# Start of a delta-rule and two-MoE kernel: loads on one queue, weight conversion ahead, unread products between small stages

## The chip, the cores and the metric

One core of a Trainium2 chip. The metric is the device time of one execution in microseconds (us); lower is better. The kernel before takes 1189.48 us, the median of three runs.

## The reference, cut to what matters

```python
# attention: batch 4, 8 heads, 768 positions, head size 48
k_n = k / (norm(k) + 1e-06)
for t in range(S):
    y[:, :, t] = einsum('bhd,bhde->bhe', q[:, :, t], state)
    v_old = einsum('bhde,bhd->bhe', state, kt)
    state = state + bt * einsum('bhd,bhe->bhde', kt, vt - v_old)
# the output, 3072 tokens x 384, goes through two MoEs
h = maximum(x @ w_in, 0.0); x = h * h @ w_out                # 384 -> 2048 -> 384
g = x @ w_gate; x = silu(g) * (x @ w_val) @ w_out2           # 384 -> 1536 -> 384
```

The weights come in 64-bit floats, everything else in 32-bit floats.

## The kernel before, in words

**Attention by blocks.** The 768 positions are 6 blocks J of 128, each of two chunks c of 64. The heads of all batches lie in two groups p. For a chunk the products of all keys (`gram`, ps_g, L360/361) are masked and scaled to a matrix M (L372, L379), and the inverse of one plus M gives the chunk's new values. For block 0 M is built in the tile NT and sent by `d_move` to the scratch d_scr (L392) and back as T (L396), where VectorE inverts 16x16 blocks (`invert16`, L474/L483); the result goes home to NT (L385, L394). TensorE then merges blocks to 32 and 64: `d_tr` (dt, ps_dt, L518), `d_merge1` (d1, ps_d), `d_merge2` (d2, ps_e), `tr11` (t11, ps_tq), `merge1` (m1, ps_m), `merge2` (m2, ps_x). After that `uu` (u, ps_u) makes the new values, `yy` (y, ps_y, L638/641) the outputs, `ku` (ps_s) the next state, and `ks` (ps_k) takes the old state's share from the values of the second chunk. `a_gram` (ps_a, L430) makes the products of queries and keys, masked by VectorE into AQ (L439). ScalarE and VectorE copy each small result from PSUM. Outputs are copied to a tile ys (L647), written to the scratch xs_scr (L650), and read back as xr by `fetch_x` (L665), for one half (256 tokens) at a time; `split_x` makes of it xh and xl (L673, L675). For blocks from 1 on, POOL inverts 32x32 blocks (`invert`, L453/L460) of M written out by `m_out` (L415) and read by `t_load` (L420).

The norms of K: `k_squares` squares on ScalarE into ps_sq and sums on VectorE (L335); `k_root` takes a root on ScalarE (L342) and eight small operations on VectorE (L344 to L351).

**Weights.** A weight is used as two pieces, hi and lo. `load_piece` (L145) loads 768 KB of raw words; ScalarE takes an absolute value (L171), VectorE does four steps on 128x768 words (L178, L180, L184, L189), ScalarE writes hi (L202), and VectorE or POOL writes lo as raw minus hi (L205). There are 16 such jobs for the first MoE, in the order w_in, w_out of a pair of column blocks m. `conv_to` does steps until a count is reached, `need` calls it before a product that wants a piece. A converted tile takes the buffer of a raw piece converted before.

**MoE units.** A unit is (J, tokens, m): ps_h (L794), ReLU and squares on ScalarE, hl on VectorE (L804), then ps_y (L820). Block 0 begins with 16 half-width units (8 values of m for each half of the tokens), all others are 512 tokens wide. Between units run the attention stages of the next block, from a list with times in units (`timed`; `spread` sets the stages of block 0's second chunk over units 0 to 5, those of `L2` over 5 to 12). Each layer takes three terms, hi times hi, hi times lo and lo times hi, so nine products a unit.

**Orders.** TensorE's and SP's instructions run in the order of the code; so do those of VectorE, POOL and ScalarE up to the first unit, and those of VectorE after it. The code's start is a list of `run`, `run_all` and `stage` calls, which fixes what stands behind what on each engine.

**Buffers.** Masks M and ys share two buffers (tag "xr"); the squares of K and, from the first unit on, ps_h share two banks (tag "h").

Of the kernel before, what the change touches and what calls it, by code (L numbers as in the profile page):

```python
# [20 lines left out]
def delta_attention_moe_moe2_kernel(  # L21
# [252 lines left out]
    def conv_to(steps, lo):  # L274

        while converted() < min(steps, STEPS * NCONV) and (making or conv1[0] in loaded or conv1[0] in begun):
            conv_one(lo)

    def need(m, kd):

        i = 2 * (m // 2) + kd + (1 if (m // 2, kd) == LAST and m % 2 else 0)
        conv_to(STEPS * (i + 1), nc.vector)
        if converted() < STEPS * (i + 2):
            flush()

# [96 lines left out]
    def d_move(c, out):
        mats = d_scr[c].rearrange("a g x s t -> (a g x) (s t)"), T0[c * 64:c * 64 + 64].rearrange("p a b -> p (a b)")
        if not out:
            nc.sync.dma_start(out=mats[0], in_=mats[1])  # L385
        for g in range(2):
            for a in range(2):
                p0 = g * 64 + a * 32
                rows = NT2[c][p0:p0 + 32, :, a * 32:(a + 1) * 32]
                blocks = d_scr[c, a, g].rearrange("x s t -> s x t")  # L390
                if out:
                    nc.sync.dma_start(out=blocks, in_=rows)  # L392
                else:
                    nc.sync.dma_start(out=rows, in_=blocks)  # L394
        if out:
            nc.sync.dma_start(out=mats[1], in_=mats[0])  # L396

    def gram(J, c, p, pool=False):
        ps = ps_t.tile([128, 8, 64], F32, tag="t", name="ps_g")
# [541 lines left out]

    def conv(n, lo=nc.vector):

        conv_to(converted() + int(STEPS * n), lo)

    P2 = range(2)

# [10 lines left out]
    for b0 in (0, 64):  # L958
# [1 line left out]
            out=mask[b0:b0 + 64], in_=mask[b0:b0 + 64], compare_op=ALU.is_ge, fill=1.0,  # L960
            base=0, pattern=[[-1, 64]], channel_multiplier=1,
        )
    for c in P2:
        k_load(1, c, nc.gpsimd)
    q_load(0, nc.gpsimd)
    run(("sq", 0, 0))
    run_all(("gram0", 0, 0, p) for p in P2)
    run(("root", 0, 0))
# [1 line left out]
    run(("mb0", 0, 0, 1, nc.gpsimd))  # L970
    run_all(("m0", 0, 0, p) for p in P2)
    run(("dmove", 0, True))
    load_w1(0, 0, nc.gpsimd)
    run(("sq", 0, 1))
    run_all(("gram0", 0, 1, p) for p in P2)
    run(("root", 0, 1))
    run(("mb0", 0, 1, 0, nc.vector))
    run(("mb0", 0, 1, 1, nc.gpsimd))
    run_all(("m0", 0, 1, p) for p in P2)
    run(("dmove", 1, True))  # L980
    load_w1(0, 1, nc.gpsimd)
    make_identity(nc, ident)
    for c in P2:
        v_load(0, c, nc.gpsimd)
    for p in P2:
        nc.gpsimd.memset(RSF[p], 0.0)
    run(("sq", 1, 0))
    load_w1(1, 0)
    run(("inv0", 0))
    run(("dmove", 0, False))  # L990
    run_all(("gram0", 1, 0, p) for p in P2)
    stage("agram", 0, 0)

    nc.vector.reduce_sum(lower, ident.rearrange("p (b z k) -> p z b k", z=2, k=16)[:, 1], axis=AX.XY)
    run(("inv0", 1))
    run(("dmove", 1, False))
    load_w1(1, 1)
    run(("root", 1, 0))
    run(("sq", 1, 1))
    run(("root", 1, 1))  # L1000
    run_all(("mb0", 1, 0, p, nc.gpsimd) for p in P2)
    merge16("dt", 0)
    run_all(("m0", 1, 0, p) for p in P2)
    run_all(("mout", 1, 0, p) for p in P2)
    merge16("d1", 0)
    run(("vn", 0, 0, nc.vector))
    run_all(("gram0", 1, 1, p) for p in P2)
    merge16("d2", 0)
    run_all(("mb0", 1, 1, p, nc.gpsimd) for p in P2)
    run_all(("m0", 1, 1, p) for p in P2)  # L1010
    run_all(("mout", 1, 1, p) for p in P2)
    run_all(("tload", 1, c) for c in P2)
    load_w1(2, 0)
    stage("t11", 0, 0)
    conv(0.5)
    stage("m1", 0, 0)
    run(("inv", 1, 0, 1, nc.gpsimd))
    conv(0.5)
    merge16("dt", 1)
    stage("m2", 0, 0)  # L1020
    conv(0.5)
    stage("u", 0, 0)
    merge16("d1", 1)
    stage("y", 0, 0)
    run(("fetch", 0, 0, TOK // 2))
    load_w1(2, 1)
    merge16("d2", 1)
    conv(0.5)
    stage("ku", 0, 0)
    stage("t11", 0, 1)  # L1030
    load_w1(3, 0)
    conv(0.5)
    run(("vn", 0, 1, nc.vector))
    stage("ks", 0, 1)
    stage("m1", 0, 1)
    stage("agram", 0, 1)
    load_w1(3, 1)
    conv(1)
    stage("m2", 0, 1)
    conv(0.5)  # L1040
    PRE = converted()
    order.close()
    order.enter_context(tc.manual_schedule(engines={mybir.EngineType.DVE, mybir.EngineType.Pool}))
# [13 lines left out]
    if True:  # L1057

        LOW2 = 300
        MID = 12  # L1060
        END = 7
        N1 = 10
        N2 = 99
        CR = 1.0
        RATE = 0.8
        LASTN = HMS[0] + 1
        seq = []
        for J in range(NJ):
            seq += [(J, c0, HT, m) for c0 in (0, HT) for m in range(HMS[J])]
            seq += [(J, 0, TOK, m) for m in range(HMS[J], NM1)]  # L1070
        L = chunk(["u"], 0, 1)
        L += [("ku", 0, 1, 0), ("y", 0, 1, 0), ("ku", 0, 1, 1), ("y", 0, 1, 1), ("fetch", 0, HT, HT)]
        L2 = [("loadq", 1), ("v", 1, 0), ("mback", 1, 0), ("mback", 1, 1), ("gap",), ("nout", 1), ("nback", 1, 0)]
        L2 += [("vn", 1, 0)] + loads(2)
        mid = MID
        GA = (5, 6, 9, 10)
        PG = []
        AA = (2, 5)
        NA = (2, 4)
        TA = 2  # L1080
# [128 lines left out]
```

## Time and profile before

| | |
|---|---|
| median of three runs | 1189.48 us (1186.06 to 1189.81) |
| the profiled execution, its own time | 1185.92 us |
| its span | 1184.1 us |
| mean granted TensorE clock | 0.946 |
| busy: PE, DVE, ACT, POOL | 92%, 55%, 33%, 23% |

The profile is one execution. "Busy" is the time an engine works; time in brackets behind a row is how long it had stood, and what ended that. The clock of TensorE is given as a share of full speed (2.4 GHz); 0.50 is the lower level, 1.2 GHz. Times of a row are from the span's start.

### The profile page before, as it was taken

The page shows a single profiled execution, that of the slowest core. Times are in us where ns is not written, and L with a number is a line of the kernel's source. Part 1 is how long each engine was busy: PE and PEld are TensorE (multiplying, and loading weights), DVE is VectorE, ACT ScalarE, POOL GpSimd, SP SyncE. Part 2 cuts the span into 40 slices and gives each one's busy share as a digit, 9 for nine tenths or more (in the row PEclk, how much of TensorE's full clock was granted, in tenths as well). Part 3 has the DMA queues.
Part 4 walks back from the last instruction along what each step waited for, and adds up shares of the span by engine and source line. Part 5 has one row for each costly group of instructions (what it writes and reads, how often), then busy time and mean ns, then how long its engine had stood idle before and what let it go on. Part 6 is the DMA issues. An engine that isn't in the chain of part 4 may idle for free. (4 is left out here: it accounts for less than half of the span.)

```text
span 1184.1 us, 25132 instructions
## 1 busy us (share of the span) xinstructions
PE 1087.6 (92%) x10863; PEld 905.3 (76%) x10863; DVE 645.5 (55%) x1116; ACT 385.2 (33%) x711; POOL 271.3 (23%) x394
## 2 busy tenths in 40 slices
PE   4378778999999999999999987899999999999998
PEld 4367667777888888788888865688888888888887
DVE  3859995456547546555543699834334343343333
ACT  1034563332233233323333666422122122122222
POOL 5067100480183166128000233300000000000000
PEclk8557887999999999999999999999999999999999
DMA  8537440461434326132211445301001010010000
GB/s 237 132 81 280 93 104 20 95 160 43 91 66 115 77 49 168 46 69 59 77 29 27 161 143 177 107 1 54 1 1 54 1 54 1 1 54 1 27 1 27
DMA packets 129119, 88.23 MB, mean 75 GB/s; under 512 B 103216, under 2 KB 107952, under 8 KB 129008
## 3 DMA queue, kind: packets, MB, share of 16 engines
q1 hardware_dynamic: 126656, 76.79, 24.6%
q0 software_dynamic: 2208, 9.57, 2.5%
q8 instruction: 85, 1.39, 0.5%
q10 hardware_dynamic: 144, 0.26, 0.1%
q14 instruction: 26, 0.21, 0.1%
HBM read 63.54 MB, written 23.07 MB: 73 GB/s over the span
## 5 line engine op out<-in xcount | busy, mean ns | idle before, releaser
L794 PE MATMUL ps_h<-xh,w 128*128 128x512 f32 (+1 forms) x684 | 215.3, 377 | 6.1 <-DVE w L205 5.5
L820 PE MATMUL ps_y<-hh,w 128*128 128x512 f32 (+1 forms) x654 | 158.5, 378 | 1.8 <-DVE w L205 1.7
L794 PEld LDWEIGHTS ps_h<-xh,w 128*128 128x128 f32 x684 | 129.9, 199 | 28.4 <-DVE w L205 6.1
L887 PE MATMUL ps_g<-x2h,w 128*128 128x512 f32 x432 | 145.9, 392 | 0.5 <-ACT x2h L872 0.5
L887 PE MATMUL ps_v<-x2h,w 128*128 128x512 f32 x432 | 144.9, 389 | 0.0
L797 ACT ACTIVATE r<-ps_h 128x512 f32<-128x512 f32 (+1 forms) x114 | 60.2, 528 | 248.0 <-PE ps_h L794 232.7
L891 DVE SCALAR_TENSOR_TENSOR th<-th,ps_g 128x512 f32<-128x512 f32 x72 | 49.4, 686 | 167.1 <-ACT th L890 166.9
L820 PEld LDWEIGHTS ps_y<-hh,w 128*128 128x128 f32 x654 | 113.4, 194 | 22.1 <-DVE w L205 2.2
L794 PE MATMUL ps_h<-xl,w 128*128 128x512 f32 (+1 forms) x342 | 126.7, 371 | 2.3 <-POOL xl L675 1.7
L800 DVE TENSOR_TENSOR r<-r 128x512 f32<-128x512 f32 (+1 forms) x72 | 50.3, 699 | 133.1 <-ACT hh L798 132.9
L912 PE MATMUL ps_o<-ph,w 128*128 128x512 f32 x432 | 111.9, 389 | 2.5 <-ACT ye L836 2.5
L820 PE MATMUL ps_y<-hl,w 128*128 128x512 f32 (+1 forms) x327 | 87.7, 378 | 18.9 <-DVE hl L804 18.9
L453 POOL TENSOR_TENSOR TMP<-T 128x30 f32<-128x30 f32 (+9 forms) x150 | 84.4, 563 | 82.5 <-DMA T<-m_scr 46.6
L890 ACT ACTIVATE th<-ps_g 128x512 f32<-128x512 f32 x72 | 43.0, 597 | 175.8 <-PE ps_g L887 175.8
L804 DVE TENSOR_TENSOR hl<-r,hh 128x512 fp32r<-128x512 f32 (+1 forms) x114 | 76.5, 671 | 43.0 <-ACT r L802 37.7
L912 PEld LDWEIGHTS ps_o<-ph,w 128*128 128x128 f32 x432 | 81.0, 188 | 19.6 <-ACT ye L836 2.9
L887 PEld LDWEIGHTS ps_g<-x2h,w 128*128 128x128 f32 x432 | 81.6, 189 | 17.9 <-ACT x2h L872 0.9
L460 POOL TENSOR_TENSOR T<-T,TMP 128x30 f32<-128x30 f32 (+9 forms) x150 | 91.9, 613 | 11.4
L887 PEld LDWEIGHTS ps_v<-x2h,w 128*128 128x128 f32 x432 | 81.2, 188 | 17.0
L894 ACT ACTIVATE ph<-th 128x512 fp32r<-128x512 f32 x72 | 45.5, 631 | 133.2 <-DVE th L892 133.2
L887 PE MATMUL ps_g<-x2l,w 128*128 128x512 f32 x216 | 84.7, 392 | 2.7 <-DVE x2l L873 2.7
L820 PEld LDWEIGHTS ps_y<-hl,w 128*128 128x128 f32 x327 | 58.9, 196 | 34.1 <-DVE hl L804 24.7
(128 smaller groups left out, 1839.3 us busy)
## 6 DMA issues: line engine op xcount, KB each, us to landing
raw<-in_moe_w_out_dram SPq DMA_DIRECT2D x12, 768.0 KB, 5.2
raw<-in_moe_w_in_dram SPq DMA_DIRECT2D x7, 768.0 KB, 9.0
m_scr<-M SPq DMA_DIRECT2D x20, 256.0 KB, 2.8
xs_scr<-ys SPq DMA_DIRECT2D x48, 96.0 KB, 2.2
xr<-xs_scr SPq DMA_DIRECT2D x12, 384.0 KB, 3.8
raw<-in_moe_w_gate_dram SPq DMA_DIRECT2D x6, 768.0 KB, 4.3
raw<-in_moe_w_val_dram SPq DMA_DIRECT2D x6, 768.0 KB, 4.4
x2raw<-y_scr SPq DMA_DIRECT2D x6, 768.0 KB, 4.6
```

What stands on the lines that cost most here:

```text
L453: eng.tensor_tensor(tmp[:, r0:r1], t_[:, r0:r1, kk:kk + 1].to_broadcast([n, r1 - r0, w]), t_[:, kk:kk + 1, kk + 1:].to_broadcast([n, r1 - ...
L460: eng.tensor_tensor(t_[:, r0:r1, kk + 1:], t_[:, r0:r1, kk + 1:], tmp[:, r0:r1], op=ALU.add)
L794: nc.tensor.matmul(ps, w_[:, kk], x_[:, kk, cols], start=n == 0, stop=n == 3 * KD - 1)
L797: nc.scalar.activation(out=r, in_=ps, func=ACTF.Relu)
L800: nc.vector.tensor_tensor(r, r, r, op=ALU.mult)
L804: eng.tensor_tensor(hl[:, at], r, hh[:, at].bitcast(F32), op=ALU.subtract)
L820: nc.tensor.matmul(acc[f], w_[:, fs], h_, start=first, stop=m == NM1 - 1 and n == 2)
L887: nc.tensor.matmul(ps, w_[:, kk], x_[:, kk], start=n == 0, stop=n == 3 * KD - 1)
L890: nc.scalar.activation(out=th, in_=gp, func=ACTF.Tanh, scale=0.5)
L891: nc.vector.scalar_tensor_tensor(out=th, in0=th, scalar=1.0, in1=gp, op0=ALU.add, op1=ALU.mult)
L894: nc.scalar.activation(out=hh, in_=th, func=ACTF.Copy)
L912: nc.tensor.matmul(o_acc[J][f], w_[:, fs], h_, start=m == 0 and n == 0, stop=m == NM2 - 1 and n == 2)
```

## The change

It touches what is issued before the first MoE unit, and one number behind it.

- The loads of K(1, 0), K(1, 1), q, V and the first two weight pieces go from POOL's queue to SP's. `d_move` is cut into `d_out`, `d_in` and `d_home`, so that other loads can stand between them.
- `make_identity` and the reduction that makes `lower` come earlier.
- `conv` counts steps, not jobs, and is called at other places: 17 steps before the first unit, 16 before.
- `warm(n)` issues n products of `ident` with itself into a tile ps_w of tag "h" that nobody reads. Ten calls make 45.
- ks, m1 and m2 of block 0's second chunk move from the list before the first unit into the timed list behind it; its a_gram stays before.
- The masks of block 1's second chunk (mb0, m0), its m_out and T, and POOL's inversion come after y of the first chunk.
- `conv_lo`, the engine of lo, is POOL's from unit 4 on, not 10, and `need` uses it too.

```diff
@@ need
-        conv_to(STEPS * (i + 1), nc.vector)
+        conv_to(STEPS * (i + 1), conv_lo[0])
@@ conv
-        conv_to(converted() + int(STEPS * n), lo)
+        conv_to(converted() + n * STEPS // 4, lo)
@@ before the list of calls
+    spare = ps_h.tile([128, 128], F32, tag="h", name="ps_w")
+    def warm(n):
+        for _ in range(n):
+            nc.tensor.matmul(spare, ident, ident, start=True, stop=True)
@@ the list of calls
-    for c in P2:
-        k_load(1, c, nc.gpsimd)
-    q_load(0, nc.gpsimd)
+    load_w1(0, 0)
+    make_identity(nc, ident)
...
-    load_w1(0, 0, nc.gpsimd)
+    load_w1(0, 1)
...
-    run(("dmove", 1, True))
-    load_w1(0, 1, nc.gpsimd)
-    make_identity(nc, ident)
-    for c in P2:
-        v_load(0, c, nc.gpsimd)
+    d_out(1)
+    conv(2)
+    run(("loadq", 0))
+    d_in(1)
...
-    run(("sq", 1, 0))
-    load_w1(1, 0)
     run(("inv0", 0))
     run(("dmove", 0, False))
-    run_all(("gram0", 1, 0, p) for p in P2)
-    stage("agram", 0, 0)
-    run(("inv0", 1))
-    run(("dmove", 1, False))
+    run(("loadk", 1, 0))
+    conv(1)
+    run(("inv0", 1))
+    stage("agram", 0, 0)
+    run(("dmove", 1, False))
+    run(("loadk", 1, 1))
+    run(("v", 0, 0))
+    load_w1(1, 0)
+    run(("sq", 1, 0))
+    warm(14)
+    merge16("dt", 0)
+    conv(3)
+    warm(4)
+    merge16("d1", 0)
...
+    warm(2)
     stage("y", 0, 0)
     run(("fetch", 0, 0, TOK // 2))
+    run_all(("mb0", 1, 1, p, nc.gpsimd) for p in P2)
+    conv(1)
+    run_all(("m0", 1, 1, p) for p in P2)
...
-    stage("ks", 0, 1)
-    stage("m1", 0, 1)
-    stage("agram", 0, 1)
     load_w1(3, 1)
-    conv(1)
-    stage("m2", 0, 1)
-    conv(0.5)
@@ the units
-        N1 = 10
+        N1 = 4
-        L = chunk(["u"], 0, 1)
+        L = chunk(["ks", "m1", "m2", "u"], 0, 1)
```

**SP's queue behind the first K loads.** Before:

```order
L392 DMA d_scr<-NT_103 32x16x32 x4
L396 DMA T_115<-d_scr 64x1024
L392 DMA d_scr<-NT_104 32x16x32 x4
L396 DMA T_115<-d_scr 64x1024
L145 DMA raw<-in_moe_w_in_dram 128x3x512
L385 DMA d_scr<-T_115 64x1024
L394 DMA NT_103<-d_scr 32x16x32 x4
```

and now:

```order
L145 DMA raw<-in_moe_w_in_dram 128x3x512
L387 DMA d_scr<-NT_103 32x16x32 x4
L392 DMA T_115<-d_scr 64x1024
L145 DMA raw<-in_moe_w_out_dram 128x2x768
L387 DMA d_scr<-NT_104 32x16x32 x4
L298 DMA AQ<-in_q_dram 48x2x1024
L299 DMA AQ<-in_q_dram 48x2x1024
L392 DMA T_115<-d_scr 64x1024
L398 DMA d_scr<-T_115 64x1024
L405 DMA NT_103<-d_scr 32x16x32 x4
```

w_in's first piece stands ahead of the writes of d_scr (NT_103 is the first chunk's matrix, T_115 the tile that is inverted); the loads of q, K and V, which were POOL's, stand behind them.

**VectorE around the inversions of block 0.** Before, from the second chunk's masked matrix to the first steps of the first inversion:

```order
L372 TENSOR_TENSOR NT_104<-mask,bB 128x512
L379 SCALAR_TENSOR_TENSOR NT_104<-ps_g,NT_104 128x512 x2
L335 TENSOR_REDUCE NS_131<-ps_sq 128x8 x2
L474 TENSOR_TENSOR TMP<-T_115 64x14 x2
L483 TENSOR_TENSOR T_115<-T_115,TMP 64x14 x2
L474 TENSOR_TENSOR TMP<-T_115 64x26 x2
```

and now, from the last step of the second inversion on:

```order
L501 TENSOR_TENSOR T_115<-T_115,TMP 64x14 x2
L502 MEMSET T_115 64x32
L457 TENSOR_TENSOR AQ<-ps_a,mask 64x8x64 x4
L336 TENSOR_REDUCE NS_131<-ps_sq 128x8 x2
L189 SCALAR_TENSOR_TENSOR raw<-raw 128x768
L178 TENSOR_SCALAR f<-f 128x768
L180 TENSOR_SCALAR f<-f 128x768
L345 TENSOR_SCALAR NS_131<-NS_131 128x16
L346 RECIPROCAL NS_131<-NS_131 128x16
```

The sums of the squares (L335, now L336) of K(1, 0) stood before both inversions, and stand behind them and the four masks of AQ (L439, now L457). One step of conversion, L184, lies between the two inversions, further up.

**TensorE ahead of the first merges, now** (before, ps_dt and ps_d stood one behind the other):

```order
L449 MATMUL ps_a<-AQ,KT 64x64
L977 MATMUL ps_w<-ident 128x128 x14
L536 MATMUL ps_dt<-ident,NT_103 32x16 x64
L977 MATMUL ps_w<-ident 128x128 x4
L550 MATMUL ps_d<-td,NT_103 32x16 x64
```

The fourteen products of ps_w come ahead of ps_dt in TensorE's order.

**VectorE in a half-width unit of the second half.** Before:

```order
L178 TENSOR_SCALAR f<-f 128x768
L180 TENSOR_SCALAR f<-f 128x768
L184 SCALAR_TENSOR_TENSOR raw<-raw,f 128x768
L189 SCALAR_TENSOR_TENSOR raw<-raw 128x768
L205 TENSOR_TENSOR w_2019<-raw,w_2019 128x6x128
L804 TENSOR_TENSOR hl<-r,hh 128x256
```

and now:

```order
L178 TENSOR_SCALAR f<-f 128x768
L822 TENSOR_TENSOR hl<-r,hh 128x256
L180 TENSOR_SCALAR f<-f 128x768
L184 SCALAR_TENSOR_TENSOR raw<-raw,f 128x768
L189 SCALAR_TENSOR_TENSOR raw<-raw 128x768
```

The lo part (L205) is no longer among VectorE's instructions; it stands in POOL's order, seven of them one behind the other.

## Rows read from the trace of the kernel before

**Rows 1.** Page, parts 1 and 2: busy time of the engines; slices of TensorE.

```profile
PE 1087.6 (92%) x10863; PEld 905.3 (76%) x10863; DVE 645.5 (55%) x1116; ACT 385.2 (33%) x711; POOL 271.3 (23%) x394
...
PE   4378778999999999999999987899999999999998
```

**Rows 2.** Windows of 10 us: length, busy us (instructions) by engine, PEclk, DMA share, GB/s.

```profile
20.00:30.00 10.00, 3.64 (x62) 3.48 (x62) 0.00 (x0) 0.00 (x0) 0.00 (x0) 0.50 0.70 235
...
50.00:60.00 10.00, 7.78 (x347) 7.41 (x348) 6.34 (x17) 2.35 (x9) 2.85 (x3) 0.50 0.75 167
...
60.00:70.00 10.00, 5.65 (x264) 5.27 (x265) 6.04 (x10) 4.09 (x7) 1.18 (x2) 0.50 0.62 113
...
70.00:80.00 10.00, 8.85 (x261) 8.34 (x259) 4.13 (x8) 1.81 (x6) 7.98 (x18) 0.50 0.26 79
...
150.00:160.00 10.00, 6.12 (x36) 5.71 (x36) 9.79 (x15) 6.66 (x13) 0.00 (x0) 0.83 0.73 195
...
190.00:200.00 10.00, 10.00 (x120) 8.18 (x119) 3.29 (x5) 2.61 (x5) 0.00 (x0) 0.71 0.11 28
```

**Rows 3.** Timeline of SP's queue: start, us, line, operation; d_scr and T.

```profile
11.01 10.22 SPq L392 DMA_DIRECT2D d_scr<-NT  x4
...
27.92 0.54 SPq L396 DMA_DIRECT2D T<-d_scr  x1
...
28.57 2.15 SPq L392 DMA_DIRECT2D d_scr<-NT  x4
...
32.90 0.46 SPq L396 DMA_DIRECT2D T<-d_scr  x1
```

**Rows 4.** Timelines of DVE, PE and ACT, 31 to 51 us; in brackets the idle time.

```profile
31.70 0.25 DVE L474 TENSOR_TENSOR TMP<-T 64x14 f32<-64x14 f32 x2 [14.44 <-DMA T<-d_scr]
...
38.21 0.65 DVE L439 TENSOR_TENSOR AQ<-ps_a,mask 64x512 f32<-64x512 f32 x1
...
49.89 1.02 DVE L335 TENSOR_REDUCE NS<-ps_sq 128x8 f32<-128x384 f32 x2
...
44.81 2.09 PE L518 MATMUL ps_dt<-ident,NT 16*32 16x16 f32 x124 [0.33 <-DMA NT<-d_scr]
...
50.95 0.22 ACT L342 ACTIVATE NS<-NS 128x16 f32<-128x16 f32 x1 [32.64 <-DVE NS L335]
```

**Rows 5.** Timelines of SP and PE: x for the two halves, first MoE product.

```profile
81.03 2.56 SPq L650 DMA_DIRECT2D xs_scr<-ys  x4
...
87.24 0.38 SPq L665 DMA_DIRECT2D xr<-xs_scr  x1
...
136.03 0.38 SPq L665 DMA_DIRECT2D xr<-xs_scr  x1
...
103.60 0.58 PE L794 MATMUL ps_h<-xh,w 128*128 128x256 f32 x1
```

**Rows 6.** Timeline of DVE in the half-width units: hl of two, L205 between.

```profile
151.37 0.42 DVE L804 TENSOR_TENSOR hl<-r,hh 128x256 fp32r<-128x256 f32 x1
...
154.76 0.95 DVE L205 TENSOR_TENSOR w<-raw,w 128x768 fp32r<-128x768 f32 x1
...
168.40 0.42 DVE L804 TENSOR_TENSOR hl<-r,hh 128x256 fp32r<-128x256 f32 x1
```

**Rows 7.** Groups by line and form on PE: ps_a in 61:104 and in 220:245.

```profile
L430 PE MATMUL ps_a<-AQ,KT 48*64 48x64 f32 x32 | 3.7, 313 | 0.0
...
L430 PE MATMUL ps_a<-AQ,KT 48*64 48x64 f32 x32 | 2.1, 220 | 0.0
```

**Rows 8.** Timelines of POOL and DVE: two inversion steps, two L205.

```profile
83.76 0.68 POOL L460 TENSOR_TENSOR T<-T,TMP 128x228 f32<-128x228 f32 x1
...
85.22 1.27 POOL L460 TENSOR_TENSOR T<-T,TMP 128x234 f32<-128x234 f32 x1
...
87.23 1.37 DVE L205 TENSOR_TENSOR w<-raw,w 128x768 fp32r<-128x768 f32 x1
...
172.20 1.02 POOL L205 TENSOR_TENSOR w<-raw,w 128x384 fp32r<-128x384 f32 x1 [24.61 <-ACT w L202]
```

More of the change, by code (lines that the diff above doesn't have):

```diff
@@ L221, in delta_attention_moe_moe2_kernel @@
     making = []
+    conv_lo = [nc.vector]
     STEPS = Piece.STEPS
@@ L379, in m0, with d_out @@
         nc.vector.scalar_tensor_tensor(out=m, in0=g0.pop((J, c, p)), scalar=-1.0, in1=m, op0=ALU.mult, op1=ALU.mult)
[L382 to L385, printed above, removed]
+    def d_out(c):
         for g in range(2):
@@ L388, in d_move, with d_in, d_home @@
                 p0 = g * 64 + a * 32
[L389 to L394, printed above, removed]
+                nc.sync.dma_start(
+                    out=d_scr[c, a, g].rearrange("x s t -> s x t"), in_=NT2[c][p0:p0 + 32, :, a * 32:(a + 1) * 32]
+                )
+    def d_in(c):
+        nc.sync.dma_start(
+            out=T0[c * 64:c * 64 + 64].rearrange("p a b -> p (a b)"),
+            in_=d_scr[c].rearrange("a g x s t -> (a g x) (s t)"),
+        )
+    def d_home(c):
+        nc.sync.dma_start(
+            out=d_scr[c].rearrange("a g x s t -> (a g x) (s t)"),
+            in_=T0[c * 64:c * 64 + 64].rearrange("p a b -> p (a b)"),
+        )
+        for g in range(2):
+            for a in range(2):
+                p0 = g * 64 + a * 32
+                nc.sync.dma_start(
+                    out=NT2[c][p0:p0 + 32, :, a * 32:(a + 1) * 32], in_=d_scr[c, a, g].rearrange("x s t -> s x t")
+                )
+    def d_move(c, out):
         if out:
-            nc.sync.dma_start(out=mats[1], in_=mats[0])
+            d_out(c)
+            d_in(c)
+        else:
+            d_home(c)
     def gram(J, c, p, pool=False):
@@ L979, in delta_attention_moe_moe2_kernel @@
     run_all(("m0", 0, 1, p) for p in P2)
-    run(("dmove", 1, True))
-    load_w1(0, 1, nc.gpsimd)
-    make_identity(nc, ident)
-    for c in P2:
-        v_load(0, c, nc.gpsimd)
+    d_out(1)
+    conv(2)
+    run(("loadq", 0))
+    d_in(1)
     for p in P2:
         nc.gpsimd.memset(RSF[p], 0.0)
-    run(("sq", 1, 0))
-    load_w1(1, 0)
+    nc.vector.reduce_sum(lower, ident.rearrange("p (b z k) -> p z b k", z=2, k=16)[:, 1], axis=AX.XY)
     run(("inv0", 0))
     run(("dmove", 0, False))
-    run_all(("gram0", 1, 0, p) for p in P2)
@@ L992, in delta_attention_moe_moe2_kernel @@
-    stage("agram", 0, 0)
-    nc.vector.reduce_sum(lower, ident.rearrange("p (b z k) -> p z b k", z=2, k=16)[:, 1], axis=AX.XY)
-    run(("inv0", 1))
-    run(("dmove", 1, False))
-    load_w1(1, 1)
-    run(("root", 1, 0))
+    run(("loadk", 1, 0))
[12 more added lines that the diff above has]
+    merge16("d1", 0)
@@ L999, in delta_attention_moe_moe2_kernel @@
+    run_all(("gram0", 1, 0, p) for p in P2)
+    run(("root", 1, 0))
+    run_all(("mb0", 1, 0, p, nc.gpsimd) for p in P2)
+    warm(2)
+    merge16("d2", 0)
+    conv(1)
+    load_w1(1, 1)
+    warm(5)
+    stage("t11", 0, 0)
+    run_all(("m0", 1, 0, p) for p in P2)
+    warm(4)
+    stage("m1", 0, 0)
+    run_all(("mout", 1, 0, p) for p in P2)
+    conv(1)
     run(("sq", 1, 1))
+    merge16("dt", 1)
+    warm(2)
+    stage("m2", 0, 0)
     run(("root", 1, 1))
-    run_all(("mb0", 1, 0, p, nc.gpsimd) for p in P2)
@@ L1002, in delta_attention_moe_moe2_kernel @@
[L1002 to L1005, printed above, removed]
     run(("vn", 0, 0, nc.vector))
+    warm(4)
+    stage("u", 0, 0)
     run_all(("gram0", 1, 1, p) for p in P2)
[L1008 to L1014, printed above, removed]
-    conv(0.5)
@@ L1016, in delta_attention_moe_moe2_kernel @@
[L1016 to L1023, printed above, removed]
+    warm(2)
     stage("y", 0, 0)
     run(("fetch", 0, 0, TOK // 2))
+    run_all(("mb0", 1, 1, p, nc.gpsimd) for p in P2)
+    conv(1)
+    run_all(("m0", 1, 1, p) for p in P2)
+    merge16("d1", 1)
+    warm(4)
+    run_all(("mout", 1, 1, p) for p in P2)
+    conv(2)
+    run_all(("tload", 1, c) for c in P2)
+    run(("inv", 1, 0, 1, nc.gpsimd))
@@ L1026, in delta_attention_moe_moe2_kernel @@
+    merge16("d2", 1)
+    warm(4)
+    conv(2)
+    load_w1(2, 0)
+    stage("ku", 0, 0)
+    stage("agram", 0, 1)
+    run(("v", 0, 1))
     load_w1(2, 1)
-    merge16("d2", 1)
-    conv(0.5)
-    stage("ku", 0, 0)
+    conv(2)
     stage("t11", 0, 1)
     load_w1(3, 0)
-    conv(0.5)
+    conv(2)
     run(("vn", 0, 1, nc.vector))
-    stage("ks", 0, 1)
-    stage("m1", 0, 1)
-    stage("agram", 0, 1)
     load_w1(3, 1)
-    conv(1)
-    stage("m2", 0, 1)
-    conv(0.5)
     PRE = converted()
@@ L1086, in delta_attention_moe_moe2_kernel @@
         clock = [0.0]
-        conv_lo = [nc.vector]
         def slot(J, n_):
```

## The prediction

> **What bounds the kernel now.** I read the busy times first. TensorE works in 92% of the span, and its row of slices is full from the eighth slice on [rows 1]; a change that touches only the start can win no more than what TensorE idles there. The windows show where that is: 190 to 200 us is the first one that is full [rows 2]. The change therefore acts through one number, the moment at which TensorE becomes continuously busy, now about 190 us. Whatever moves it moves the end by as much; whatever is won earlier and lost again before it is worth nothing.
>
> Two stretches lie before it. In the first (to 104 us) a serial chain runs: masked gram matrices, inversion on VectorE, merges, state, output, then x for the first MoE. The timeline of the queues shows its stations. The four d_scr writes are issued at 11.01, but the load of T that needs them starts only at 27.92 [rows 3], and VectorE stands 14.44 us for it [rows 4]. The second round of the same writes goes out at 28.57 and its T load at 32.90, after 4.33 us [rows 3]. ScalarE stands until 50.95 for a square root, while ps_dt had ended at 44.81 + 2.09 = 46.90 [rows 4]; the copy td and all the merges are behind that. The granted clock is at its lower level, 0.50, all through this chain [rows 2]. The load of x for the first half is issued at 87.24 and the first MoE product runs at 103.60 [rows 5]. In the second stretch (104 to 190 us) the sixteen half-width units of the first block run, and VectorE, which converts the weights, is the bound: 9.79 of 10 us busy at 150 to 160 while TensorE has 6.12 [rows 2]. The writes of hl, one a unit, go from 151.37 to 168.40 in four units, 4.26 us each [rows 6].
>
> **The change, part by part.**
>
> *Loads on one queue.* The K, q, V and first weight loads leave POOL's queue and are issued by SP, most of them behind the d_scr writes that they used to keep company; only w_in piece 0 stays ahead. If the writes then take 4.33 us as in the second round, T is issued at 15.3 and not at 27.92, 12.6 us earlier. If piece 0 (0.79 MB, at the 235 GB/s of the window of the old wait [rows 2], 3.3 us) still lies wholly in front, 9.3. The lower bound is 0, if other traffic holds the writes all the same. I take 12, since piece 0 is issued while VectorE still builds the matrices. The Trainium skill, "DMA: Bandwidth & Descriptors", section "Issuing engines are not separate DMA queues", says that the DMAs of all issuing engines run on the same 16 DMA engines and interleave, and that several issuers save only issue time; by it one queue wins nothing as such, and only the new order does. The late T load beside the loads of the other queue agrees with that.
>
> *Unread products.* 45 float32 products of 128x128 are put between the small stages. The trace has none; the nearest rows are the grams ps_a, 64 columns: 32 records in 3.7 us at the lower clock and in 2.1 at the upper [rows 7], two records to a product. Twice the columns make 0.46 and 0.26 us a product, so all 45 cost 12 to 21 us of TensorE, much of it in gaps where it waits for copies.
>
> The first 14 are another matter. They write a bank that the squares of K(1,0) used, so they wait until VectorE has reduced these, and in VectorE's new order that is behind both inversions. VectorE starts at 31.70 - 12 = 19.7; inversion 6.5 (31.70 to 38.21), one conversion step 1.0, inversion 6.5, four masks of 0.65, two reduces 1.0 [rows 4]: 37.3. Fourteen products at the lower clock, 6.4 us, put ps_dt at 43.7, against 44.81. Of the 12 us, **1.1 is left**.
>
> *ScalarE's root.* The last root now stands far behind dt and d1 of the first chunk, so td no longer waits from 46.90 to 50.95: **4.1 us** [rows 4].
>
> *Small stages from d1 to y.* TensorE worked 7.78 + 5.65 + 8.85 = 22.3 us in 50 to 80 [rows 2]; at the upper clock a third less by the means of ps_a (313 to 220 ns [rows 7]), 6.6. Against it 23 of the unread products lie here, 6 to 11 us if none fits into a gap. So the gain is from -11 (clock down, no gap) to +6.6 (clock up, all in gaps); in between, with half in gaps and the clock up for most of it, **+2**. x for the first half is then asked for about 7 us earlier, near 80.
>
> *Masks of the second chunk of block 1* take their two buffers now after ys, not before it, and VectorE, in its order, waits there until the x writes have read ys. That took from 81.03 to 87.24 [rows 5], so up to 6 us in which conversion stands; 0 if it has other work ahead. POOL's inversion of block 1 starts about as much later than before; it is read only with the stages of block 1 at the end of the half-width units, so I cost it at nothing, and if that cover were gone TensorE would show a gap just before its full stretch.
>
> *Stages ks, m1, m2 of the second chunk* move from before the first MoE product into its first units. The first product comes earlier by that too: x near 80 instead of 87, no 9 us of stages behind it, so about 87 against 103.60. But the second half's x needs these stages, and they now queue between converted weights. From the first product to that x's load took 136.03 - 103.60 = 32.4 us [rows 5]. The same eight units, with 3 us of moved scaling and subtraction, 9 us of stages and up to 6 of the mask wait, make 41 to 50: the load would be asked for at 128 to 137. Against 136.03 the gain is -1 to 8; I take **+3.5**, the middle.
>
> *Lo parts on POOL.* From the fifth unit on the subtraction L205 goes to POOL, seven there and not two. VectorE loses 0.95 us a unit [rows 6]; five whole ones give **+4.75**, if POOL keeps up. It shows 1.02 us for half the width [rows 8], so 2.04 for the whole. A lo must end before ScalarE's next hi (0.9) can take its slot; 2.94 a unit together, below the 3.3 that VectorE then needs. If VectorE is blocked once a unit, by the 1.37 - 0.95 = 0.42 of [rows 6, 8], 2.6 is left; twice, 0.5.
>
> *One more step of conversion* ahead of the MoE (17 quarter-jobs and not 16): one step, **+0.9**, which is all VectorE's.
>
> Sum: 3.5 + 4.75 + 0.9 = 9.15 earlier. The profiled execution took 1185.92; the median of three is 1189.48, 3.56 above it. 1185.92 - 9.15 = 1176.8, in terms of the median 1180.3. I forecast 1180.0.
>
> **The rivals.**
>
> *A. The clock comes up early and stays.* If the unread products lift it ahead of d1 and it holds, the small stages gain all of their 6.6, nearly 5 more than I took, and a full clock in the first units keeps TensorE's stages from adding to VectorE's queue: the second half starts 8 to 10 us earlier, and with the pace term the whole is 14 to 20, about 1172. For it: the clock is low where windows are part empty [rows 2]. Against it: at 150 to 160 it is 0.83 in the middle of real work.
>
> *B. Nothing is left.* The 14 waiting products, the mask wait and the moved stages eat the early gain, and hi and lo in turn set the pace of the second half: gain 0 to 3, about 1188. For it: the second half's x hangs on work that was moved behind the first product.
>
> *C. Slower: POOL's lo parts collide with VectorE.* While POOL was at the inversion, an operation of 0.68 took 1.27 beside VectorE's work, and an L205 took 1.37 [rows 8] where it takes 0.95 alone [rows 6]. If every lo of 2.04 is doubled to 4.1, then hi 0.9, lo 4.1 and 0.2 between them make 5.2 us a unit against 4.26, over seven units +6.6; with the early gain gone as in B the median comes to 1195. It decides from a lo of 3.2 us on, where the cycle is as long as the old pace. The Trainium skill, "SBUF — State Buffer", section "Who interferes with whom", calls the port pair of VectorE and GpSimd an exclusive lock, the second one fully blocked for the whole instruction. By it a lo waits for each VectorE operation of two SBUF inputs that came first, and the sum would go towards C, 1195; rows 8 agree that the two engines stretch each other.
>
> **How the numbers follow.** Forecast 0.50, A 0.20, B 0.16, C 0.14. A measurement of this kernel tells differences from about 0.3%, 3.6 us, so the limits are 1185.9 and 1193.1. The forecast's own range, from its bounds (start of the second half -1 to 8, pace 0.5 to 4.75), is 1175 to 1188. With the middle of A, all of B, and of C what comes out mildly, the range is 1168 to 1191; that leaves out A's fast end and most of C. Faster: 0.47 of the forecast, all of A, 0.05 of B: 0.72. Same: 0.03, 0.10 of B and 0.02 of C: 0.15. Slower: 0.13.
>
> **What would show each step.** T's load issued near 15 to 18 us and VectorE's inversion from about 20; fourteen ps_w products at about 37 and ps_dt not before 43; no ScalarE wait for a root ahead of td; the first ps_h near 87; the second half's x load within 128 to 137; POOL's lo rows of 2.0 to 2.6 us and the hl writes 3.3 to 3.6 apart in the last units; and the first full window of TensorE about 9 us earlier. The prediction is wrong in its chain if ps_dt comes well before 42 or after 48, in its pace if the lo rows are 3.2 us or longer, and in its sum if TensorE's full stretch still begins within 3 us of 190.

## The result and the profile after

The changed kernel takes 1199.55 us, the median of ten runs (1193.22 to 1202.41); the kernel before, in ten runs, 1184.78. The ratio is 1.0111, with a 95% interval of 1.0089 to 1.0133: about 13 us slower, where 9 us faster was forecast. 1199.55 lies outside the range of 1168 to 1191. (The three runs behind the 1189.48 of the forecast all lie above the median of the ten.)

The page, busy time and the slices of TensorE, for [rows 1]:

```profile
PE 1091.7 (91%) x10953; PEld 908.5 (76%) x10953; DVE 647.6 (54%) x1106; ACT 385.5 (32%) x715; POOL 287.6 (24%) x390
...
PE   2685848999999999999999987999999999999998
```

TensorE has 4.1 us more busy time and 12 us more span. The windows of 10 us (length, busy us and instructions of PE, PEld, DVE, ACT, POOL; PEclk, DMA share, GB/s), for [rows 2]:

```profile
40.00:50.00 10.00, 9.34 (x280) 8.91 (x283) 2.40 (x4) 1.55 (x4) 0.00 (x0) 0.73 0.91 268
50.00:60.00 10.00, 6.45 (x229) 5.94 (x219) 1.71 (x9) 0.89 (x4) 2.04 (x2) 0.61 0.12 45
60.00:70.00 10.00, 8.38 (x314) 7.63 (x308) 7.17 (x14) 4.50 (x11) 0.00 (x0) 0.84 0.23 57
...
150.00:160.00 10.00, 2.29 (x9) 2.10 (x10) 6.06 (x8) 1.82 (x4) 9.22 (x16) 0.56 0.82 156
...
190.00:200.00 10.00, 5.36 (x95) 5.04 (x97) 6.92 (x20) 4.37 (x12) 1.01 (x1) 0.60 0.01 2
200.00:210.00 10.00, 10.00 (x143) 8.64 (x140) 6.41 (x16) 2.88 (x7) 0.00 (x0) 0.88 0.12 29
```

The first full window is 200 to 210, not 190 to 200. The granted clock did rise in the chain (0.61 to 0.84 against 0.50). The first full-width hl tells the shift to the hundredth: before and after (timeline of VectorE),

```profile
198.06 0.69 DVE L804 TENSOR_TENSOR hl<-r,hh 128x512 fp32r<-128x512 f32 x1 [4.49 <-ACT r L802]
```

```profile
208.12 0.69 DVE L822 TENSOR_TENSOR hl<-r,hh 128x512 fp32r<-128x512 f32 x1 [2.81 <-ACT r L820]
```

10.06 us of the 12.2 us between the two spans are lost ahead of it; I use this station below and call it **the mark**. The rest appears between 660 and 674 us. Where the 10 us come from is read in the timeline of SP's queue, for [rows 3, 5]:

```profile
12.68 2.41 SPq L387 DMA_DIRECT2D d_scr<-NT  x4
...
16.62 0.52 SPq L392 DMA_DIRECT2D T<-d_scr  x1
...
90.20 0.38 SPq L683 DMA_DIRECT2D xr<-xs_scr  x1
...
146.31 0.38 SPq L683 DMA_DIRECT2D xr<-xs_scr  x1
```

T is asked for 11.3 us earlier than before, x of the first half 3.0 us later, x of the second half 10.3 later. So 14.3 us are lost between T and the first x (the 11.3 gained and 3.0 more), and 7.3 more between the two halves. Behind the second x the loss first grows, to 14.7 us at the fifth hl write of the second half (168.40 became 183.13). Some 4.6 us of it come back just ahead of the mark, between the last half-width hl (187.37, now 202.02) and the first full-width one; TensorE works there without a pause in both kernels, at a mean granted clock of 0.61 before and 0.98 now. TensorE's waits by 33 to 86 us (view of waits: line, waited for, us in total, times, longest) show the first part. Before:

```profile
PE ps_d L532 <- ACT td L523: 4.5, 1, 4.5
PE ps_tq L564 <- issue: 1.9, 1, 1.9
PE ps_x L592 <- issue: 1.8, 1, 1.8
PE ps_dt L518 <- issue: 1.0, 1, 1.0
```

After:

```profile
PE ps_w L977 <- DVE NS L336: 7.5, 1, 7.5
PE ps_d L550 <- issue: 3.5, 1, 3.5
PE ps_x L610 <- issue: 2.4, 1, 2.4
PE ps_u L631 <- DVE V L308: 2.4, 1, 2.4
PE ps_dt L536 <- issue: 0.8, 1, 0.8
```

The wait for td is gone, as forecast. In its place stand the unread products' wait for the sums of the squares, 3.5 us at the same ps_d put down to issue, and 2.4 us for the scaling of V, which VectorE does behind a root that ScalarE gives late. TensorE also has more to do: from ps_dt to the end of the outputs y (44.81 to 82.07 before, 45.87 to 86.08 now) it works 30.6 us and not 26.4, and stands for 9.6 and not 10.8. The unread products take 10.1 us there. The gram of K(1, 0) takes some 3.3: before, it ran ahead of ps_dt, and now it runs behind ps_d, so that this stretch has 128 records of ps_g where it had 64.

The second part is VectorE's, between the first ps_h (103.60, now 98.44) and the second half's load of x. Windows of that stretch, before and after, in the columns of [rows 2], each with one of VectorE's groups by line and form (count, busy us, mean ns, idle):

```profile
103.60:136.03 32.43, 26.29 (x318) 24.07 (x316) 31.34 (x47) 20.64 (x37) 8.95 (x14) 0.90 0.31 98
...
L178 DVE TENSOR_SCALAR f<-f 128x768 f32<-128x768 f32 x6 | 3.6, 600 | 0.1
```

```profile
98.44:146.31 47.87, 33.77 (x518) 30.50 (x513) 44.56 (x58) 23.55 (x47) 41.15 (x49) 0.79 0.59 203
...
L178 DVE TENSOR_SCALAR f<-f 128x768 f32<-128x768 f32 x6 | 5.0, 839 | 0.0
```

The stretch takes 15.4 us more, and VectorE is busy 13.2 us more in it. About half of that is work that now falls into it, the masks of AQ (2.7 us) foremost. The other half, some 6 us by the means and counts of five groups, is that VectorE's steps and hl writes take longer while POOL is at the inversion, which is busy 41.2 us here and not 9.0: L178 839 ns and not 600, L184 1209 and not 959, L205 1214 and not 1021. POOL, first and last step of the inversion, and what stood behind it:

```profile
101.39 0.25 POOL L471 TENSOR_TENSOR TMP<-T 128x30 f32<-128x30 f32 x1 [10.00 <-DMA T<-m_scr]
...
157.24 0.16 POOL L480 MEMSET T<- 128x32 f32 x1
157.31 2.10 POOL L693 TENSOR_TENSOR xl<-xr,xh 128x256 fp32r<-128x256 f32 x3
...
164.48 1.94 POOL L205 TENSOR_TENSOR w<-raw,w 128x768 fp32r<-128x768 f32 x1 [1.02 <-ACT w L202]
```

The inversion ran from 101.4 to 157.2 (56 us, 42.8 before), in the middle of the half-width units, and xl of the second half, behind it in POOL's order, came at 157.3; by the view of the tile xl TensorE stood 7.1 us for it. That wait lies behind the second half's load of x, so it is no part of the 7.3. Ahead of the first x, VectorE waited for the root (12.2 us, to 54.6) and for the masks (7.5 us, to 90.1; view of waits of VectorE, 33 to 200 us):

```profile
DVE NS L345 <- ACT NS L343: 12.5, 2, 12.2
DVE M L380 <- POOL M L373: 8.2, 2, 7.5
```

In the units of the second half the groups of VectorE by line and form show the price of the lo parts. Before (151 to 171 us; count, busy us, mean ns, idle):

```profile
L205 DVE TENSOR_TENSOR w<-raw,w 128x768 fp32r<-128x768 f32 x6 | 5.7, 950 | 0.0
...
L184 DVE SCALAR_TENSOR_TENSOR raw<-raw,f 128x768 int32<-128x768 int32 x4 | 3.8, 960 | 0.1
```

After (163 to 187 us):

```profile
L184 DVE SCALAR_TENSOR_TENSOR raw<-raw,f 128x768 int32<-128x768 int32 x4 | 10.0, 2508 | 0.1
```

L205's 950 ns are gone and L184 takes 1548 ns more: it starts while POOL's lo is running and ends about 0.8 us after that (at 167.24, the lo at 166.42). POOL's lo itself takes 1.94. The hl writes stand 4.9 us apart (168.74 to 173.64) where it was 4.26 [rows 6].

### The profile page after: what moved, and what is told of

It reads as the page before. It is cut to its first block, busy times and chain, and to the rows that moved or that the text cites. A ratio compares the mean times of both kernels' runs of the same rounds, so it can differ in the third digit from the quotient of the medians.

```text
span 1196.3 us, 25313 instructions
## 1 busy us (share of the span) xinstructions
PE 1091.7 (91%) x10953; PEld 908.5 (76%) x10953; DVE 647.6 (54%) x1106; ACT 385.5 (32%) x715; POOL 287.6 (24%) x390
## 5 line engine op out<-in xcount | busy, mean ns | idle before, releaser
L812 PE MATMUL ps_h<-xh,w 128*128 128x512 f32 (+1 forms) x684 | 212.0, 372 | 3.6 <-DVE w L205 2.0
L812 PEld LDWEIGHTS ps_h<-xh,w 128*128 128x128 f32 x684 | 127.1, 195 | 25.2 <-DVE w L205 2.2
L471 POOL TENSOR_TENSOR TMP<-T 128x30 f32<-128x30 f32 (+9 forms) x150 | 92.7, 618 | 82.4 <-DMA T<-m_scr 71.2
L478 POOL TENSOR_TENSOR T<-T,TMP 128x30 f32<-128x30 f32 (+9 forms) x150 | 96.6, 644 | 11.4
```

The lines of the kernel that those rows point to most:

```text
L471: eng.tensor_tensor(tmp[:, r0:r1], t_[:, r0:r1, kk:kk + 1].to_broadcast([n, r1 - r0, w]), t_[:, kk:kk + 1, kk + 1:].to_broadcast([n, r1 - ...
L478: eng.tensor_tensor(t_[:, r0:r1, kk + 1:], t_[:, r0:r1, kk + 1:], tmp[:, r0:r1], op=ALU.add)
L812: nc.tensor.matmul(ps, w_[:, kk], x_[:, kk, cols], start=n == 0, stop=n == 3 * KD - 1)
```

## The experiments

Ratios are to the kernel before, run beside each; 0.001 is 1.2 us. The changed kernel's is 1.0111. Edits are to the changed kernel unless said.

**e1, no unread products.**

```diff
-        for _ in range(n):
+        for _ in range(0):
             nc.tensor.matmul(spare, ident, ident, start=True, stop=True)
```

> The changed kernel with the 45 unread products left out, all else as changed. Theory Q (POOL's queue: its inversion of block 1 starts 30 us later than before, stretches VectorE's work in the half-width units, holds xl of the second half, and the lo parts then block VectorE's L184): the chain to x comes earlier by what the products held up, 5 to 8 us (x load at 82 to 85 and not 90.2), everything behind moves by as much, the inversion still ends after xl is wanted; 1191 to 1195 against the changed kernel's 1199.5. Theory U (the unread products are the loss): x load at 78 or earlier and the whole loss of 15 us gone, 1185 or less. Third view (the clock): without them the stages run at 0.50 and x comes later than 90.

Measured: 1187.23 us, ratio 1.0025 (1.0003 to 1.0047). The mark is at 194.77, 13.35 us ahead of the changed kernel and 3.3 ahead of the one before. x of the first half is asked for at 75.80. U is nearest, though its 1185 was not reached: the products carry most of the loss. The third view fell, since x came earlier and not later. The late inversion and the lo parts stay (xl at 143.2, hl 4.9 apart), so they are paid for here too, out of the earlier T. The gain at the mark did not last: by 300 us this kernel was 2.5 us behind the one before, with granted clocks of 0.73 at 230 to 240 and 0.66 at 270 to 280, where the kernel before has 1.00 and 0.96.

The waits of TensorE in 33 to 86, the two largest:

```profile
PE ps_u L631 <- DVE V L308: 4.4, 1, 4.4
PE ps_m L600 <- ACT tq L574: 4.2, 1, 4.2
```

**e2, lo parts on VectorE to unit 9.**

```diff
-        N1 = 4
+        N1 = 10
```

> The changed kernel with the lo parts on VectorE up to unit 9, as before (one number, 4 back to 10). Theory Q: VectorE's L184 falls from 2.52 to 0.96 us in units 8 to 13, the hl writes stand 4.3 and not 4.9 us apart, 3 to 4 us are won: 1196. Theory U: no difference, since the loss lies ahead of these units. If the lo parts cost nothing on POOL, 3 to 4 us slower.

Measured: 1194.92, ratio 1.0089 (1.0067 to 1.0111); the mark at 204.08, 4.04 earlier than in the changed kernel, and L184 in these units back to

```profile
L184 DVE SCALAR_TENSOR_TENSOR raw<-raw,f 128x768 int32<-128x768 int32 x4 | 3.8, 960 | 0.1
```

So moving the lo parts cost about 4 us at the mark and did not win 4.75. The intervals of the two whole times overlap a little; the row and the mark decide.

**e3, POOL's inversion ahead of y.** mb0 of (1, 1) goes ahead of the scaling of V, its gram ahead of u, and m0, m_out, T's load and the inversion behind u, before y:

```diff
+    run_all(("mb0", 1, 1, p, nc.gpsimd) for p in P2)
     run(("vn", 0, 0, nc.vector))
+    run_all(("gram0", 1, 1, p) for p in P2)
     stage("u", 0, 0)
+    run_all(("m0", 1, 1, p) for p in P2)
+    run_all(("mout", 1, 1, p) for p in P2)
+    run_all(("tload", 1, c) for c in P2)
+    run(("inv", 1, 0, 1, nc.gpsimd))
```

> The changed kernel with the masks of block 1's second chunk, their write, the load of T and POOL's inversion put back ahead of the outputs y of the first chunk; the same number of unread products. Theory Q: the inversion starts at 80 to 88 and not at 101, ends at 125 to 135, xl of the second half no longer waits for POOL (7.1 us of TensorE's wait gone), the first units are stretched by the inversion all the same; 6 to 10 us faster, 1190 to 1193. Theory U: at most 2 us.

Measured: 1201.39, ratio 1.0142 (1.0108 to 1.0176): no gain. POOL now waits for xl's input, and not the other way round:

```profile
154.11 2.50 POOL L693 TENSOR_TENSOR xl<-xr,xh 128x256 fp32r<-128x256 f32 x3 [18.83 <-ACT xh L691]
```

but x of the first half is asked for at 92.82 and not 90.20, since the masks' writes and T's loads stand ahead of those of ys in SP's queue. Theory Q, as I put it, fell: the place of the inversion alone is worth nothing here. It still runs beside the half-width units, from 90.22 on.

**e4, the loads back on POOL's queue** (K(1), q, the first chunk of V, first two pieces; the rest as changed; for instance)

```diff
-    load_w1(0, 0)
+    for c in P2:
+        k_load(1, c, nc.gpsimd)
+    q_load(0, nc.gpsimd)
...
```

> The changed kernel with the loads of K(1), q, V and the first two weight pieces back on POOL's queue at their old places. If the early T (20 and not 32 us) still reaches the end: 6 to 10 us slower, 1206 to 1209. If it is lost on the way, at the unread products and the root, within 3 us of the changed kernel.

Measured: 1205.21, ratio 1.0176 (1.015 to 1.0202), 7.7 us slower than the changed kernel by the ratios. VectorE's inversion starts at 29.99 and not 20.26, 9.7 us later. The delay shrinks from station to station: 7.5 us at ps_dt (53.35), 5.2 at the first x (95.38), 3.4 at the mark (211.56). So the loads' new place gains, and a part of it, 3.4 us by the mark and 7.7 by the ratios, reaches the end. Queue and order were changed together; which of the two gains is not shown.

**e5, the first 14 products left out, the other 31 kept.**

```diff
-    warm(14)
     merge16("dt", 0)
```

> The changed kernel without the first 14 unread products; the other 31 stay. View W (the loss is the wait of the first 14 for VectorE's reduction): ps_dt starts near 33 and not 45.9, as without any of them, and 12 to 13 us of the 13.4 that the leaving out of all 45 won come back: first ps_h near 86, 1187. View S (each of the other 31 costs too, since they stand in line and not in gaps): 8 to 9 come back, first ps_h near 90, 1191. View C (the others pay, by the clock): more than all of it, first ps_h before 84, 1185 or less.

Measured: 1193.52, ratio 1.006 (1.0036 to 1.0085); the mark at 203.31. ps_dt runs at 33.8, but the next four products then wait for the same sums, and ps_d behind them starts at 41.6:

```profile
39.61 2.08 PE L977 MATMUL ps_w<-ident 128*128 128x128 f32 x8 [3.96 <-DVE NS L336]
```

View W expected 1187 and had overlooked this: the wait is that of the bank, and whichever product comes first has it. View S is near in number (first ps_h at 91.64 against 90), but the row shows the wait, and not the others' own cost.

**e6, the first 14 ahead of the squares.**

```diff
+    warm(14)
     run(("sq", 1, 0))
-    warm(14)
     merge16("dt", 0)
```

> The changed kernel with the first 14 unread products issued ahead of the squares of K(1,0), so that they no longer wait for VectorE's reduction; all 45 stay. View W: they run from 32 to 38, ps_dt at 38.5 to 39, 7 us earlier than in the changed kernel, and so is the first ps_h: 91 and 1192 to 1193. If the amount of products counts and not the wait: within 2 us of the changed kernel's 1199.5.

Measured: 1187.52, ratio 1.0033 (1.001 to 1.0055), not to be told from e1 without any products. The mark is at 197.13, 11.0 us ahead of the changed kernel.

```profile
32.24 4.39 PE L977 MATMUL ps_w<-ident 128*128 128x128 f32 x28
36.55 1.33 PE L536 MATMUL ps_dt<-ident,NT 16*32 16x16 f32 x128
```

One line moved by one place gives back some 9 us of the 13. What costs here is the wait, then, and much less the 45 products: against e1 they cost 2.4 us at the mark. In the mended kernel they cost more (e10).

**e7, mended**: e1 and e2 together, the scaling of V ahead of the root of (1, 1), and one conversion step moved to behind the 32-merges.

```diff
     merge16("d2", 0)
-    conv(1)
...
     run_all(("mout", 1, 0, p) for p in P2)
-    conv(1)
+    run(("vn", 0, 0, nc.vector))
+    conv(2)
...
     run(("root", 1, 1))
-    run(("vn", 0, 0, nc.vector))
```

> The changed kernel without unread products, lo parts on VectorE to unit 9, the scaling of V ahead of the root of (1,1), and one conversion step moved from ahead of the 32-merges to behind them (so that ScalarE does not wait 4 us for a weight load ahead of tq). Theory Q and W together: 4 us of the lo parts, 4 of V's scaling and 3 to 4 of ScalarE's wait on top of the kernel without unread products (1187.2): full stretch of TensorE 10 to 14 us ahead of the kernel before, 1174 to 1180. If gains at the start are given back later by the clock (as 5 us were without unread products between 225 and 330): 1180 to 1185.

Measured: 1181.38, ratio 0.9969 (0.9947 to 0.9991): 3.7 us faster than the kernel before. The mark is at 187.73, 10.3 ahead of the kernel before; 4 us of that are given back by 300 us. Of the two waits mended, V's is gone; the end of the merge ps_x is at 59.4 us against 58.9 in e1, since other waits at issue (2.6 at ps_e, 2.65 at ps_m, 1.9 at ps_dt) took the place of the 4.2 for tq.

**e8, mended, with the inversion ahead of y** (e7 and e3).

> The last kernel with POOL's inversion put back ahead of y as well. Theory Q: xl of the second half no longer behind the inversion, 2 to 4 us better than the last one. As the inversion alone won nothing (1201.4), the other view: 0 to 3 us worse, because SP's queue holds the writes of ys behind those of the masks.

Measured: 1178.09, ratio 0.9947 (0.9923 to 0.997), the fastest of all here. The mark is at 186.35, 11.7 ahead of the kernel before, and this time 11 us of it reach the end of the profiled execution. By the whole times e7 and e8 can't be told apart surely; the inversion's place, worth nothing in e3, is worth 1.4 us at the mark here. The stations show why it is so little. With the inversion early (76.1 to 122.3) the stretch between the two loads of x takes 52.0 us and not 56.7 as in e7, and TensorE's wait for xl falls from 6.9 to 1.5 us; but the first x is asked for 5.3 us later (78.66 against 73.36), behind the masks' writes in SP's queue.

**e9, weight loads later.** From e8:

```diff
-    load_w1(1, 0)
     run(("sq", 1, 0))
...
     merge16("d2", 0)
-    load_w1(1, 1)
...
     run_all(("mout", 1, 0, p) for p in P2)
+    load_w1(1, 0)
+    load_w1(1, 1)
     run(("vn", 0, 0, nc.vector))
-    conv(2)
...
     stage("u", 0, 0)
+    conv(2)
```

> The mended kernel with the early inversion, and with the loads of the weight pieces (1,0) and (1,1) issued behind the masks' write (about 55 us) and not at 43; the two conversion steps that need them behind u. View F (TensorE's waits put down to issue, 8.8 us between 33 and 86 in that kernel, are its instructions being fetched on the engines that the loads fill): they shrink by 3 us or more at 38 to 58, x is asked for 2 to 4 us earlier (75 to 77 and not 78.7), 1175 to 1177 against 1178.1. If these waits are TensorE's own and the loads do not matter: they stay at 8 to 9 us and the time within 2 us.

Measured: 1181.41, ratio 0.9966 (0.9943 to 0.9989), not faster. The waits at issue are the point. In e8 (timeline of TensorE):

```profile
53.31 1.01 PE L600 MATMUL ps_m<-tq,NT 32*32 32x32 f32 x31 [3.19 <-issue]
57.23 0.62 PE L536 MATMUL ps_dt<-ident,NT 16*32 16x16 f32 x32 [1.65 <-issue]
```

In e9:

```profile
49.84 1.02 PE L600 MATMUL ps_m<-tq,NT 32*32 32x32 f32 x31 [0.18 <-issue]
54.04 0.62 PE L536 MATMUL ps_dt<-ident,NT 16*32 16x16 f32 x32 [1.92 <-issue]
61.55 0.36 PE L362 MATMUL ps_g<-KT 48*64 48x64 f32 x1 [3.50 <-issue]
```

The 3.2 us at ps_m are gone and 3.5 have appeared at ps_g, in the stretch where the moved loads now run (issued at 51.71 and 53.51). In that wait lie a busy DMA and one 16 KB packet of instructions (view of DMA, 58.1 to 61.5: busy tenths in 40 slices, and the queue):

```profile
DMA  9999989998999745254301002002000100000000
...
q8 instruction: 1, 0.02, 1.8%
```

So in these two kernels the long wait at issue stands where the loads run. Shorter waits, of 1.6 to 2.0 us, stay, and in sum the waits at issue are 9.2 us where e8 had 8.8. x of the first half did not come earlier, for another reason: ScalarE's copies of ys waited 4.57 us for the masks' write to end, td stands behind them in ScalarE's order, and TensorE waited 6.7 us for td (ps_e). From the timeline of ScalarE:

```profile
75.66 0.60 ACT L665 ACTIVATE ys<-ps_y 128x512 f32<-128x512 f32 x1 [4.57 <-DMA m_scr<-M]
...
77.10 0.62 ACT L554 ACTIVATE td<-ps_d,lower 128x128 f32<-128x128 f32 x2
```

The rows speak for view F's cause of the long waits, without showing it (the conversion steps were moved too); the sum stayed as the other view had it, and the gain did not come.

**e10, e8 with all 45 products**, the first 14 placed as in e6.

> The mended kernel with the early inversion, with all 45 unread products in it, the first 14 ahead of the squares of K(1,0). View C (they pay by the clock where they don't wait): granted clock of 33 to 86 up from about 0.6 to 0.8, TensorE's small stages 30% shorter, 1174 or less. View F (at the upper clock the stages are held by the fetch of instructions, so the clock gives little, and the products take room): x is asked for 1 to 4 us later, 1178 to 1182.

Measured: 1182.7, ratio 0.9973 (0.9955 to 0.9992), with the mark 6.1 us behind that of e8. Windows of 33 to 86 us, e8 and e10:

```profile
33.00:86.00 53.00, 38.39 (x1418) 36.17 (x1419) 34.97 (x92) 14.37 (x38) 12.75 (x21) 0.60 0.56 153
```

```profile
33.00:86.00 53.00, 46.23 (x1430) 43.40 (x1430) 30.73 (x85) 13.69 (x35) 8.21 (x14) 0.71 0.48 120
```

The products raise the mean granted clock from 0.60 to 0.71, and the chain is later all the same: x of the first half is asked for at 84.65 against 78.66. View C fell. View F has the time, all but 0.7 us, but its cause is not shown: TensorE works 7.8 us more in this stretch (46.23 against 38.39), and that work is enough to account for the delay.

## Why the prediction was wrong, step by step

Forecast and mark are 19.2 us apart (9.15 earlier against 10.06 later). 13.8 of them arise ahead of the second half's load of x (146.3 against 132.5): 2.2 up to ps_dt, 8.0 from there to the first x, 1.2 to the first ps_h, 2.4 to the second x. The other 5.4 arise behind it.

*T earlier by 12.* Right: 27.92 became 16.62, VectorE began at 20.26.

*The first 14 products hold ps_dt to 43.7.* Right in mechanism, small in size: the sums ended at 40.4, not 37.3. The second inversion stood until 29.76 for its own T, whose load is behind those of q in SP's queue. ps_dt ran at 45.87. The products took 5.84 us against 6.4 expected. I had seen this cost, 11 us of the 12, and still called it a part of a gain, while e6 shows that it is the largest single loss.

*ScalarE's root, +4.1, and the small stages, +2.* **This is the step that failed first.** I counted the wait for td as won and asked only what the products cost in line; I did not ask what is late next on TensorE, VectorE and ScalarE at each later stage. From ps_dt to the load of x took 44.3 us (45.87 to 90.20) where I had 36 and the kernel before 42.4. Waits took the place of the one for td, 3.5 and 2.4 us at issue and 2.4 for V, and up to the end of y TensorE had 4.1 us more work. I had left out the gram of K(1, 0), some 3.3 us. The products took 10.1 us, near the top of my 6 to 11, and not half of that in gaps, since TensorE's idle time fell by 1.2 us only. Without any products (e1) the way to x still takes 42.8 us, with more idle time (12.6 us up to the end of y, 10.8 before): so the products alone are not the reason. The upper clock was granted for much of the chain, which I had hoped for, but the products and the gram took up what it saved. (Before, too, the clock was not at 0.50 all through: the window 80 to 90 has 0.84.)

*The masks, up to 6 us.* Right in mechanism, a little over the bound: VectorE stood 7.55 for M, and M for the x writes. But this lay ahead of the first product (to 90.06), and not between it and the second x, where my sum had it.

*POOL's later inversion, cost nothing.* **This is the second step that failed.** I named as cover that its result is read only at the end of the half-width units. But its 30 pairs of steps now ran beside VectorE's work in the units, where VectorE is the bound, and lengthened it by some 6 us. And POOL's order has xl of the second half right behind it, which I had not costed; TensorE waited 7.1 us for that. e3 won nothing at the mark by an earlier inversion and e8 1.4 us, since the first x then comes later; e8's 4.7 us between the two loads of x bear the cost out, but no run shows it alone.

*Second half's x at 132.5.* It came at 146.3. From the first ps_h (98.44, not 87) it took 47.9 us, inside the 41 to 50 that I gave; 11.4 of the 13.8 us are those of the steps before. That the 47.9 fits is partly luck: the wait for the masks, which I had in it, fell elsewhere, and the lengthening by POOL, which I did not have, took its place.

*Lo parts on POOL, +4.75.* **The third step that failed, in sign.** POOL did keep up, at 1.9 to 2.0 us each, as estimated. But I let the block fall on the lo or cost VectorE 0.42, where it falls on VectorE's L184 and costs 1.55 in each unit: 0.95 won, 1.55 lost. e2 shows 4 us at the mark. The trace of the kernel before had shown this, further on, where the weights of the second MoE are converted with their lo parts on POOL:

```profile
669.25 1.99 POOL L205 TENSOR_TENSOR w<-raw,w 128x768 fp32r<-128x768 f32 x1 [13.47 <-ACT w L202]
...
669.53 2.52 DVE L184 SCALAR_TENSOR_TENSOR raw<-raw,f 128x768 int32<-128x768 int32 x1
```

The L184 just before it, at 665.87 and with no lo beside it, took 0.96. I had looked at such pairs in the start alone. The Trainium skill, "SBUF — State Buffer", section "Who interferes with whom", says that the order of issue, and not the shape of the operation, decides which of the two is blocked, for the whole instruction. By it L184, which starts second, stands until the lo is done: the trace agrees, 2508 ns against 960. In rival C I had assumed the other order, with POOL as the one that waits.

*The rivals.* C, with 0.14, had the sign, by luck: the time ends above the point it named (1195), but its mechanism, a doubled lo, is not what happened. B's three causes (waiting products, masks, moved stages) are all in the rows and more than ate the early gain; only the first was undone in a run. Three separate losses had been seen, and each was set off against a hoped gain; slower deserved far more than 0.13.

At the mark, leaving out the products is worth 13.4 us and moving the lo parts back 4.0, while undoing the loads costs 3.4. Each was undone alone, and they don't add up to the 10.1; what each changes in the others was not separated. The moved stages (ks, m1, m2) and the new place of the gram of K(1, 0) were undone in no run.

The last 2.5 us, at 660 to 674 (first weights of the second MoE), appear as 1.7 to 2.3 us in e2, e3, e4, e6 and e10, all with the first 14 products, and as at most 0.3 in e1, e5, e7, e8 and e9, all without them. In the changed kernel VectorE stands there 5.83 us for ScalarE's first step and not 3.30, and ScalarE 3.15 and not 0.62 for the first weights' load, which SP issues at 670.53 and not at 658.65, 2.4 us more than the shift of 9.5. Why it is issued so late is open.

## What to carry to other kernels

When a wait is taken out, write down for each engine what its next instruction in order waits for, since the chain will stop there: here three other waits of 2 to 4 us stood behind the one removed. Filler work on an idle engine must own its buffer and wait for nothing; one place in the order decided some 9 us. Even then it was not free: in e10 it cost 6 us. Before work is moved to POOL beside VectorE, look which of the two starts second in each pair, and look in the old trace at what such a pair already costs each of them.

## What the runs showed of the hardware

A lo part of 1.94 us on POOL lengthened a VectorE operation of two inputs from 960 to 2508 ns and was itself hardly lengthened: the lo at 161.57, which ran almost wholly while VectorE stood (until 163.08), took 1.89. That the loss is so one-sided I had not expected. An operation of one input is lengthened as well: beside a lo of half width, L178 or L180 on 128x384 took 0.93 to 1.18 us where it takes 0.35 (at 172.25 in the kernel before, 187.54 in the changed one, 173.31 in e1, 163.42 in e8).

TensorE's long idle times put down to issue go with the weight loads. In the changed kernel one packet of 16 KB of instructions lies in the 3.5 us wait that ended at 53.78 (view of DMA, 50.3 to 53.7):

```profile
DMA  9999958432320800000000000000000000000000
...
q8 instruction: 1, 0.02, 1.9%
```

and in e9, with the weight loads moved, such a wait stood elsewhere. That the packet is TensorE's and waits behind the loads is what both rows suggest; neither that nor the order inside a DMA engine was measured.

A higher granted clock did not pay for the products that came with it: the mean of 33 to 86 us rose from 0.60 to 0.71 between e8 and e10, TensorE worked 7.8 us more there, and x was asked for 6 us later.
